# Chunk attention and two feed-forward layers: token blocks of 4x512 + 256 in place of 6x384, first block in one pass, two product buffers

## The chip, the core and the metric

The kernel runs on one core of one Trainium2 chip. The metric is the device time of a run in microseconds (us), shown as the median of three runs. A profiled execution of the same program gives the rows below; its span is counted from the first to the last instruction.

The engines are PE (TensorE, matrix products; PEld are its weight loads), DVE (VectorE), ACT (ScalarE), POOL (GpSimd) and SP, which issues the DMA transfers. Each engine works through its own list of instructions in order, and they meet at semaphores.

## What is computed

There are 2304 tokens (4 sequences of 576), 512 features and 2048 hidden features. Attention is local: each chunk of 64 tokens sees itself alone, with 8 heads of 64 features. Two feed-forward layers follow, the first with softplus, the second with a rational function.

```python
scores = scale * np.matmul(q_c, k_c.transpose(0, 1, 2, 4, 3))   # chunks of 64 tokens
attn = np.exp(scores - scores.max(-1)); attn = attn / (attn.sum(-1) + 1e-09)
x = np.matmul(attn, v_c)                      # -> (2304, 512)
h = x @ w_in                                  # (2304, 2048), layer one
x = (np.maximum(h, 0) + np.log1p(np.exp(-np.abs(h)))) @ w_out
h = x @ w_in2                                 # layer two
P = a[0] + a[1]*h + a[2]*h**2 + a[3]*h**3
Q = 1.0 + abs(b[0])*abs(h) + abs(b[1])*h**2
out = (P / (Q + 1e-6)) @ w_out2
```

## The kernel before

**Products.** Each operand of a product is held as a rounded part and a remainder, and a product is three terms (TERMS): rounded with rounded, rounded with remainder, remainder with rounded. The hidden features are cut into 16 chunks of 128 (fc), the tokens into 6 blocks of T = 384 (three tiles of 128 each). A step s is one chunk of one block. In products_h (L719) it has 12 matmuls of 384 columns into a PSUM tile h. From h, the engines make g, the activation split in two parts: in layer one, softplus twice on ACT (L753 the whole, L758 the rounded part) and a subtraction on POOL (L761); in layer two the rational function on ACT and DVE, then the copy on ACT (L284) and the subtraction on POOL (L292) of split. Then come the output products: products_out1 (L858), 12 matmuls of 384 columns, or products_out2 (L886), 9 matmuls of 512 columns, since in layer two a matmul takes 128 tokens as weights and the 512 output features as columns. They add up in PSUM over the 16 chunks.

**Buffers.** The pool gpool holds three tiles g, ps_h two tiles h, raw four tiles for loads. PSUM holds two sums of 2x512 columns (ps_acc) and one such tile for attention (ps_att). In layer two the attention tile becomes the third sum and one of the two places for the squares.

**Weights.** They lie in memory as 64-bit floats. For each chunk, w_in's and w_out's 512 KB are loaded, scaled down on ACT (L342, "magnitudes"), put together on DVE (L348, L357) and split (L284 on ACT or L286 on POOL, then L292 on DVE). The magnitudes of layer one need another ACT table than softplus has, so each pair of weights costs two table loads (L258).

**Passes.** Blocks 0 and 1 go through layer one in half passes of 8 chunks (HALF): block 0 with chunks 0 to 7, block 1 with the same, then both with chunks 8 to 15. The sums of the first half go to memory (part) and are added in evac1 after the second.

**Attention.** Tiles 0 to 2 are worked on before the first step; tiles 0 to 5 are loaded early into places that weights take later. Their q, k and probabilities are transposed on PE (L491, L591) and copied by ACT (L503, L615). Tiles 6 to 17 are transposed on DVE in 32x32 blocks (L516, L606; 32 instructions a tile), and are worked on during the steps of the blocks ahead of theirs.

**Order.** The program writes down tasks with costs and dependencies (add), and Program.schedule sets each engine's order by them: a list scheduler that goes backward and forward some rounds and keeps its best. The costs only set the order. Dummy matmuls (keep_warm, L1142) fill PE's planned gaps before the first step.

Of the kernel before, what the change touches and what calls it, by code (L numbers as in the profile page):

```python
# [11 lines left out]
F32 = mybir.dt.float32  # L12
# [11 lines left out]
T = 384  # L24
HALF = 8
# [4 lines left out]
CONVERTED = (1,)  # L30
# [5 lines left out]
DIVIDE_BY_POOL = set()  # L36
E_BY_VECTOR = set(range(6, 18))


class Program:  # L40
# [15 lines left out]
    def __init__(self):  # L56
        self.tasks, self.deps, self.table, self.part = [], [], [], ("", 0)
        self.writer, self.readers, self.last_alloc = {}, {}, {}
# [128 lines left out]
def tile_chunk_attention_two_ffn(  # L187
# [30 lines left out]
    NB = NT // T  # L218
    NTB = T // TB
# [16 lines left out]
    att_stack = ctx.enter_context(ExitStack())  # L236
    ps_att = att_stack.enter_context(tc.tile_pool(name="ps_att", bufs=1, space=PSUM))
# [9 lines left out]
    HEAD = 4 * HALF  # L247
# [67 lines left out]
    def prepare(name, after, signed):  # L315
        layer, which, fc = name
        prog.part = f"convert {layer}", f"{which}{fc}"
# [52 lines left out]
    def complete(name, rkey, mkey, shift, merge, signed):  # L370
        layer, which, fc = name
        prog.part = f"convert {layer}", f"{which}{fc}"
# [23 lines left out]
    def reload_w(which, fc):  # L396
# [4 lines left out]
        prog.part = "reload", f"{which}{fc}"  # L401
# [27 lines left out]
    BY_VECTOR = 2 * NTB  # L429
    EARLY = 2 * NTB  # L430
    qk_t, v_t, room = {}, {}, {}

    def attention(tb):
        first = tb < NTB
        j, part = divmod(tb, NTB)
        prog.part = "attention", tb
        qkey = turn("wi", FC) if tb < EARLY else turn("raw", 4)
        vkey = turn("wo", FC) if tb < EARLY else "v"
# [3 lines left out]
        def load_qk(n):  # L442
# [3 lines left out]
            def f():  # L446
                if tb >= EARLY and n == 0:
                    qk_t[tb] = raw.tile([P, H, 2, D], F32, tag="raw", name=f"qk_{tb}")
                for off, m, b, s in runs(tb * TB, TB):
                    if tb < BY_VECTOR:  # L450
# [15 lines left out]
        def load_v():  # L466
            if tb >= EARLY:
                v_t[tb] = att1.tile([P, H, D], F32, tag="v", name=f"v_{tb}")
# [178 lines left out]
        name = min(tb, NTB)  # L647
        ke = ("e", name)
        ka = ("aT", name)
        km, ks = turn("mx", 4), turn("sm", 4)  # L650
        turned = [("turned", name, n) for n in range(16)]
        for n in range(2):
# [3 lines left out]
                alloc=None if tb < EARLY else "raw",  # L656
            )
        qks = [qkey, (qkey, 0), (qkey, 1)]
        if tb < BY_VECTOR:
            for n in range(2):  # L660
# [6 lines left out]
                    turned[8 * n : 8 * n + 8] if n else turned,  # L667
                    alloc=None if first else "qkT",
                )
        else:  # L670
            for n in range(16):
                add(
                    DVE, 0.45, turn_blocks(n // 8, n // 4 % 2, n // 2 % 2, n % 2), qks,
                    [turned[n]] if n else turned, alloc="qkT",
# [12 lines left out]
        if tb in DIVIDE_BY_POOL:  # L687
            add(POOL, 1.0, divide, [ke, ks], [ke])
        else:
            add(DVE, 0.6, divide, [ke, ks], [ke])  # L690
        if tb in E_BY_VECTOR:
            kas = [(ka, n) for n in range(16)]
            for n in range(16):
                add(
                    DVE, 0.315, turn_e_blocks(n // 4, n % 4), [ke],
                    [kas[n]] if n else [ka, *kas], alloc="aT",
                )
        else:
            kas = [ka]
            add(PE, 0.46, turn_e, [ke], [b0])  # L700
            add(ACT, 0.48, take_e, [b0], [ka], alloc="aT")
        add(PE, 0.78, values, [ka, *kas, (vkey, 0)], [b0, b1])
# [6 lines left out]
    def products_h(layer, s, fc, j):  # L709

        key = turn("h", 2)
        prog.part = "h" if s < HEAD else "later h", s

        def f():
            ps = ps_h.tile([P, 512], F32, tag="h", name=f"h_{layer}_{s}")
            hs[s] = ps[:, :T]
# [8 lines left out]
        parts = range(NTB) if layer == 1 else range(KC)  # L725
        reads = [(wk, 0), (wk, 1)] + [((xkey[layer, j], c), n) for c in parts for n in range(2)]
        add(PE, 2.085, f, reads, [key], alloc="h")
        return key

    def scratch(s):  # L730
        t = {}

        def new(tag):
            t[tag] = tmp.tile([P, T], F32, tag=tag, name=f"{tag}_{s}")
# [4 lines left out]
    def split_g(s, t, key, reads):  # L739
        def alloc():  # L740
            gs[s] = gpool.tile([P, 2, T], F32R, tag="g", name=f"g_{s}")

        split(lambda n: gs[s][:, n], lambda: t["t2"], ACT, POOL, T, reads, key, "g", alloc)

    def softplus(s, hkey):

        t, new = scratch(s)
        prog.part = "g" if s < HEAD else "later g", s
        kl, kg = turn("t2", 2), turn("g", 3)
# [5 lines left out]
        def hi():  # L755
            table(SOFTPLUS)
            gs[s] = gpool.tile([P, 2, T], F32R, tag="g", name=f"g_{s}")
            act.activation(gs[s][:, 0], hs[s], AF.Softplus)  # L758

        def lo():  # L760
            pool.tensor_tensor(  # L761
                out=gs[s][:, 1], in0=t["t2"], in1=gs[s][:, 0].bitcast(F32), op=ALU.subtract
            )

        add(ACT, 0.37, whole, [hkey], [kl], alloc="t2", table=SOFTPLUS)
        add(ACT, 0.37, hi, [hkey], [(kg, 0)], alloc="g", table=SOFTPLUS)
        add(POOL, 1.09, lo, [kl, (kg, 0)], [(kg, 1)])
        return kg

    def rational(s, hkey, start=None):  # L770

        t, new = scratch(s)
        prog.part = "g" if s < HEAD else "later g", s
        ku = ("att", 1) if s % 2 == 0 else (x["ukey"], 0)
        kd, kp, kg = turn("t1", 2), turn("t2", 2), turn("g", 3)
        bring = {0: "att", 1: "acc"}.get(start)  # L780

        def u():
            return (x["even"] if s % 2 == 0 else x["u"][:, 0])[:, :T]

        def square():
            if bring == "att":
                att_stack.close()
                ps_two = ctx.enter_context(tc.tile_pool(name="ps_two", bufs=1, space=PSUM))
                for what in ("third", "even"):
                    x[what] = ps_two.tile([P, 512], F32, tag=what, name=what)  # L790
            if bring == "acc":
                x["u"] = ps_acc.tile([P, 2, 512], F32, tag="acc", name="u")
# [25 lines left out]
        add(
            ACT, 0.56,
# [366 lines left out]
```

## Time and profile before

| what | value |
|---|---|
| median of the runs | 894.42 us (894.19 to 894.69) |
| span of the profiled execution | 892.4 us |
| PE busy | 868.6 us (97%), 5642 matmuls |
| PEld busy | 811.7 us (91%) |
| DVE busy | 680.2 us (76%) |
| ACT busy | 522.5 us (59%), of it 44.9 us in 35 table loads |
| POOL busy | 269.2 us (30%) |
| DMA | 74.38 MB, mean 83 GB/s |

The run is 2.0 us longer than the span of the profiled execution. Matmuls are pipelined: each is shown some 340 ns long, while the next begins 173 ns after it, so the pace is read from the starts. A busy PE is therefore not yet PE at its pace. Wait tables name who released an engine last.

### The profile page before, as it was taken

What the parts mean: (1) busy time and instruction counts of PE and PEld (TensorE: products, weight loads), DVE (VectorE), ACT (ScalarE), POOL (GpSimd) and SP (SyncE); (2) the same over time, 40 slices, a digit from 0 to 9 for tenths busy, and PEclk for the clock granted to TensorE, in tenths of its full rate; (3) what the DMA queues carried; (4) which work ended last, traced back from release to release, by engine and by line L of the source; (5) the groups of instructions that cost most, each with busy time, mean ns of one, the idle gap of its engine ahead of it and who ended that gap; (6) DMA issues with size and microseconds to landing.
All of it is one profiled execution on the core that took longest, in us unless ns stands there. A gap on an engine that the chain in (4) does not pass through costs nothing. (4 is left out here: it accounts for less than half of the span.)

```text
span 892.4 us, 14897 instructions
## 1 busy us (share of the span) xinstructions
PE 868.6 (97%) x5642; PEld 811.7 (91%) x5642; DVE 680.2 (76%) x1326; ACT 522.5 (59%) x991; POOL 269.2 (30%) x278
## 2 busy tenths in 40 slices
PE   8898999999999999999998999999999999999997
PEld 7788999999999999999997889898889888888996
DVE  4686679899779969922598887877787687787885
ACT  4799972243233333234447877766677767776774
POOL 0124431222122122215334935225224225222221
PEclk9999999999999999999999999999999999999999
DMA  9755573141443434134353412002000000000000
GB/s 189 212 179 206 179 206 84 48 119 40 116 118 95 108 94 131 49 118 139 122 175 123 134 54 71 1 1 69 3 1 24 12 1 1 36 1 1 36 0 36
DMA packets 77353, 74.38 MB, mean 83 GB/s; under 512 B 34272, under 2 KB 62944, under 8 KB 77280
## 3 DMA queue, kind: packets, MB, share of 16 engines
q1 hardware_dynamic: 77280, 73.42, 28.4%
q8 instruction: 44, 0.72, 0.4%
q14 instruction: 29, 0.24, 0.1%
HBM read 58.20 MB, written 15.20 MB: 82 GB/s over the span
## 5 line engine op out<-in xcount | busy, mean ns | idle before, releaser
L858 PE MATMUL acc<-g,w_1o 128*128 128x384 f32 x1152 | 218.2, 337 | 3.7 <-POOL g L761 3.3
L719 PE MATMUL h<-xT,w_2i 128*128 128x384 f32 x1152 | 216.5, 337 | 1.9 <-DVE t L796 1.8
L719 PE MATMUL h<-xT,w_1i 128*128 128x384 f32 x1152 | 213.2, 336 | 2.7 <-ACT w_1i L284 2.7
L719 PEld LDWEIGHTS h<-xT,w_2i 128*128 128x128 f32 x1152 | 204.0, 188 | 11.2 <-DVE t L796 5.0
L858 PEld LDWEIGHTS acc<-g,w_1o 128*128 128x128 f32 x1152 | 200.5, 188 | 6.0 <-POOL g L761 3.8
L719 PEld LDWEIGHTS h<-xT,w_1i 128*128 128x128 f32 x1152 | 199.9, 188 | 4.5 <-ACT w_1i L284 3.6
L761 POOL TENSOR_TENSOR g<-t,g 128x384 fp32r<-128x384 f32 x96 | 103.0, 1073 | 272.7 <-ACT g L758 206.3
L292 POOL TENSOR_TENSOR g<-t,g 128x384 fp32r<-128x384 f32 x96 | 97.9, 1020 | 253.5 <-ACT g L284 191.5
L886 PE MATMUL acc<-w_2o,g 128*128 128x512 f32 x576 | 148.4, 392 | 0.9 <-POOL g L292 0.6
L886 PEld LDWEIGHTS acc<-w_2o,g 128*128 128x128 f32 x576 | 107.4, 188 | 23.0 <-POOL g L292 0.9
L753 ACT ACTIVATE t<-h 128x384 f32<-128x384 f32 x96 | 46.8, 490 | 101.5 <-PE h L719 96.5
L758 ACT ACTIVATE g<-h 128x384 fp32r<-128x384 f32 x96 | 47.1, 490 | 70.2 <-PE acc L858 52.8
L516 DVE STREAM_TRANSPOSE qkT<-qk 32x256 f32<-32x256 f32 x192 | 83.8, 436 | 4.8 <-PE aps L534 1.2
L886 PE MATMUL third<-w_2o,g 128*128 128x512 f32 x288 | 82.8, 394 | 1.4 <-POOL g L292 1.4
L284 ACT ACTIVATE g<-t 128x384 fp32r<-128x384 f32 x96 | 50.0, 521 | 45.9 <-DVE t L796 42.1
L829 DVE TENSOR_TENSOR t<-h,t 128x384 f32<-128x384 f32 x96 | 53.2, 554 | 26.2 <-ACT t L815 13.8
L820 ACT ACTIVATE t<-h,na_t 128x384 f32<-128x384 f32 x96 | 64.2, 669 | 12.2 <-PE h L719 7.0
L796 DVE SCALAR_TENSOR_TENSOR t<-t,na_t,h 128x384 f32<-128x384 f32 x96 | 58.7, 612 | 12.6 <-ACT t L815 4.0
L886 PEld LDWEIGHTS third<-w_2o,g 128*128 128x128 f32 x288 | 53.1, 188 | 10.9 <-POOL g L292 2.8
L815 ACT ACTIVATE t<-h,b_t 128x384 f32<-128x384 f32 x96 | 54.9, 573 | 9.8 <-PE h L719 6.2
L606 DVE STREAM_TRANSPOSE aT<-e 32x128 f32<-32x128 f32 x192 | 58.1, 303 | 3.1
L258 ACT ACT_TABLE_LOAD x35 | 44.9, 1283 | 1.3 <-PEq L1167 0.7
(92 smaller groups left out, 914.9 us busy)
## 6 DMA issues: line engine op xcount, KB each, us to landing
wr_1i<-in_moe_w_in_dram SPq DMA_DIRECT2D x16, 512.0 KB, 3.8
wr_1o<-in_moe_w_out_dram SPq DMA_DIRECT2D x16, 512.0 KB, 4.4
wr_2i<-in_moe_w_in_dram SPq DMA_DIRECT2D x16, 512.0 KB, 3.9
wr_2o<-in_moe_w_out_dram SPq DMA_DIRECT2D x16, 512.0 KB, 4.3
x<-x2s SPq DMA_DIRECT2D x12, 384.0 KB, 2.7
x2r<-x SPq DMA_DIRECT2D x12, 384.0 KB, 3.3
out_dram<-o SPq DMA_DIRECT2D x18, 256.0 KB, 2.1
qk<-in_q_dram SPq DMA_DIRECT2D x16, 256.0 KB, 5.1
```

The source lines that it names most:

```text
L284: act.activation(d, s, AF.Copy)
L292: eng.tensor_tensor(out=dst(1), in0=src(), in1=dst(0).bitcast(F32), op=ALU.subtract)
L516: vec.transpose(tiles["qkT"][p0 : p0 + 32, n, :, c * CH : (c + 1) * CH].rearrange("p g (u t) -> p g t u", t=2), qk_t[tb][p1 : p1 + 32, h:: ...
L606: vec.transpose(o[32 * k : 32 * k + 32, :, 32 * p : 32 * p + 32], e[32 * p : 32 * p + 32, :, 32 * k : 32 * k + 32],)
L719: pe.matmul(hs[s], w[:, a, c * P : (c + 1) * P], xt[:, b, c, :], start=n == 0, stop=n == 3 * KC - 1,)
L761: pool.tensor_tensor(out=gs[s][:, 1], in0=t["t2"], in1=gs[s][:, 0].bitcast(F32), op=ALU.subtract)
L796: return lambda: vec.scalar_tensor_tensor(out=out(), in0=in0(), scalar=scalar, in1=in1(), op0=op0, op1=op1)
L815: ACT, 0.465, lambda: (table(EXP_LN), act.activation(new("t1"), h(), AF.Abs, scale=b_t[:, 0:1])),
L820: lambda: act.activation(new("t2"), h(), AF.Identity, scale=na_t[:, 3:4], bias=na_t[:, 2:3]),
L829: DVE, 0.47, lambda: vec.tensor_tensor(out=p(), in0=h(), in1=p(), op=ALU.mult),
L858: pe.matmul(accs[run, half][:, c % 2, :T], wts[1, "o", fc][:, a, c * P : (c + 1) * P], gs[s][:, b, :], start=first and n == 0, stop=last a ...
L886: pe.matmul(sum2(j, c), gs[s][:, b, c * P : (c + 1) * P], wts[2, "o", fc][:, a, :], start=first and n == 0, stop=last and n == 2,)
```

## The change

The tokens are cut into four blocks of 512 and one of 256 (tokens 2048 to 2303, attention tiles 16 and 17). Layer one takes them in the order 0, 4, 1, 2, 3, layer two in 0, 1, 4, 2, 3. Each block goes through all 16 chunks at once; the half passes, their sums in memory and the additions are gone. Tiles 0 to 3 come before the first step, 16 and 17 are the other two that are loaded early. The tiles transposed by DVE are 6 to 15 (ten in place of twelve); 4, 5, 16 and 17 are transposed by PE. gpool has two tiles in place of three. The results of a sum go out through tiles of the raw pool, 2x512 at a time, in place of a tile of their own (iop). In layer two the squares lie in the attention tile, and both sums of ps_acc hold two token tiles each. Later attention tiles use the pool of the activations (tmp, t1). A step's output products are put on the scheduler's list one step after it in place of two; the costs of tasks follow the block's size.

```diff
-T = 384
-HALF = 8
+T = 512
+BLOCKS = ((0, 512), (512, 512), (1024, 512), (1536, 512), (2048, 256))
+ORDER1 = (0, 4, 1, 2, 3)
+ORDER2 = (0, 1, 4, 2, 3)
-E_BY_VECTOR = set(range(6, 18))
+STARTING = (0, 1, 2, 3)
+STAGED = (0, 1, 2, 3, 16, 17)
+QK_BY_VECTOR = set(range(6, 16))
+E_BY_VECTOR = set(range(6, 16))
...
-    gpool = ctx.enter_context(tc.tile_pool(name="gpool", bufs=3))
+    gpool = ctx.enter_context(tc.tile_pool(name="gpool", bufs=2))
-    iop = ctx.enter_context(tc.tile_pool(name="iop", bufs=1))
...
     def products_h(layer, s, fc, j):
         key = turn("h", 2)
+        n_tok = BLOCKS[j][1]
...
-                    hs[s], w[:, a, c * P : (c + 1) * P], xt[:, b, c, :],
+                    hs[s], w[:, a, c * P : (c + 1) * P], xt[:, b, c, :n_tok],
...
+    def evacuate(layer, j, half, n, store, store_cost, outs):
+        name = layer, j, half
+        key = turn("raw", 4)
...
-    passes = [
-        (0, range(0, HALF), 0),
-        (1, range(0, HALF), 0),
-        (0, range(HALF, FC), 1),
-        (1, range(HALF, FC), 1),
-    ] + [(j, range(FC), 2) for j in range(2, NB)]
...
+    for bi, j in enumerate(ORDER1):
+        last_block = bi == len(ORDER1) - 1
+        coming = [] if last_block else [t for t in tiles_of(ORDER1[bi + 1]) if t not in STAGED]
...
+            if coming and fc % 4 == 0:
+                attention(coming.pop(0))
...
             hkey = products_h(1, s, fc, j)
             steps.append(len(prog.tasks) - 1)
-            gkey = softplus(s, hkey)
+            if len(outs) > 1:
+                outs.pop(0)()
+            gkey = softplus(s, hkey, j)
...
-            if len(outs) > 2:
-                flush()
```

DVE before the first step: in the kernel before, one weight and the products xT of tiles 1, 2 (aps_1, aps_2) and 3, which belongs to block 1 (xT_1).

```order
L584 TENSOR_TENSOR e_3_362<-e_3_362,sm_3_388 128x512
L292 TENSOR_TENSOR xT_0_283<-aps_2_215,xT_0_283 128x4x128
L348 TENSOR_SCALAR cm_1i_0_448<-cm_1i_0_448 128x512
L292 TENSOR_TENSOR xT_1_450<-aps_3_309,xT_1_450 128x4x128
L357 SCALAR_TENSOR_TENSOR cm_1i_0_448<-wr_1i_0_385,cm_1i_0_448 128x512
L292 TENSOR_TENSOR w_1i_0_126<-cm_1i_0_448,w_1i_0_126 128x512
```

The same place now:

```order
L584 TENSOR_TENSOR room_3_1_137<-room_3_1_137,sm_3_389 128x512
L351 TENSOR_SCALAR cm_1i_0_393<-cm_1i_0_393 128x512
L360 SCALAR_TENSOR_TENSOR cm_1i_0_393<-wr_1i_0_344,cm_1i_0_393 128x512
L296 TENSOR_TENSOR w_1i_0_120<-cm_1i_0_393,w_1i_0_120 128x512
L296 TENSOR_TENSOR xT_0_290<-aps_2_246,xT_0_290 128x4x128
L296 TENSOR_TENSOR xT_0_290<-aps_3_311,xT_0_290 128x4x128
```

The weight's three instructions stand ahead of the last two products, and all four products belong to block 0, whose first step reads them.

PE where the first half pass ended; h_1_8 is layer one, step 8, w_1i_0 the first chunk of w_in, acc_0_0 the first sum of the first pass:

```order
L719 MATMUL h_1_7_931<-xT_0_283,w_1i_7_133 128x384 x12
L858 MATMUL acc_0_0_569<-g_6_922,w_1o_6_929 128x384 x6
L719 MATMUL h_1_8_963<-xT_1_450,w_1i_0_126 128x384 x12
L719 MATMUL h_1_9_985<-xT_1_450,w_1i_1_127 128x384 x12
L719 MATMUL h_1_10_1011<-xT_1_450,w_1i_2_128 128x384 x12
L858 MATMUL acc_0_1_586<-g_6_922,w_1o_6_929 128x384 x6
```

The same steps now:

```order
L716 MATMUL h_1_7_923<-xT_0_290,w_1i_7_127 128x512 x12
L863 MATMUL acc_1_0_0_547<-g_6_918,w_1o_6_916 128x512 x6
L863 MATMUL acc_1_0_1_561<-g_6_918,w_1o_6_916 128x512 x6
L716 MATMUL h_1_8_972<-xT_0_290,w_1i_8_128 128x512 x12
L863 MATMUL acc_1_0_1_561<-g_7_967,w_1o_7_965 128x512 x6
L863 MATMUL acc_1_0_0_547<-g_7_967,w_1o_7_965 128x512 x6
```

Step 8 went back to the first chunk with another block's tokens; now it takes the ninth chunk (w_1i_8) for the same block, and each step's output products stand one step behind it.

PE in layer two, third block, before:

```order
L719 MATMUL h_2_139_6929<-xT2_2_5858,w_2i_11_5287 128x384 x12
L886 MATMUL third_5197<-w_2o_8_5156,g_136_6908 128x512 x3
L886 MATMUL acc2_5328<-w_2o_8_5156,g_136_6908 128x512 x6
L719 MATMUL h_2_140_6971<-xT2_2_5858,w_2i_12_5376 128x384 x12
L886 MATMUL acc2_5328<-w_2o_9_5235,g_137_6944 128x512 x6
```

And in the block of 256 now:

```order
L716 MATMUL h_2_118_6269<-xT2_4_5540,w_2i_6_4386 128x256 x12
L889 MATMUL acc_2_4_0_6175<-w_2o_3_4254,g_115_6249 128x512 x6
L716 MATMUL h_2_119_6306<-xT2_4_5540,w_2i_7_4437 128x256 x12
L889 MATMUL acc_2_4_0_6175<-w_2o_4_4307,g_116_6282 128x512 x6
L716 MATMUL h_2_120_6343<-xT2_4_5540,w_2i_8_4495 128x256 x12
```

A step's output products still stand three steps behind it, with two buffers g; the matmuls of a step are 12 of 256 and 6 of 512 columns.

## Rows read from the trace of the kernel before

**Rows 1.** Stretches of the span: PE, PEld, DVE, ACT, POOL busy; clock; DMA.

```profile
33.70:90.00 56.30, 49.98 (x363) 46.19 (x360) 42.53 (x70) 53.15 (x78) 18.88 (x20) 1.00 0.57 190
...
120.00:188.80 68.80, 68.43 (x575) 66.01 (x573) 62.77 (x147) 25.17 (x45) 16.98 (x17) 1.00 0.33 86
...
440.00:500.00 60.00, 56.48 (x303) 54.05 (x302) 54.92 (x87) 39.12 (x78) 29.48 (x29) 0.97 0.48 150
500.00:886.60 386.60, 383.65 (x1915) 344.51 (x1915) 301.30 (x552) 276.33 (x560) 127.36 (x135) 1.00 0.07 23
```

**Rows 2.** PE in order of time, first 70 us, attention and the first step.

```profile
29.84 1.04 PE L491 MATMUL aps<-ident,qk 128*128 128x128 f32 x8
30.71 1.06 PE L1142 MATMUL warm<-ident 128*128 128x128 f32 x8
32.63 1.15 PE L534 MATMUL aps<-qkT 64*64 64x64 f32 x32 [0.86 <-ACT qkT L503]
33.71 4.49 PE L719 MATMUL h<-xT,w_1i 128*128 128x384 f32 x24
...
62.22 0.69 PE L622 MATMUL aps<-aT,v 64*64 64x64 f32 x32
62.85 2.35 PE L719 MATMUL h<-xT,w_1i 128*128 128x384 f32 x12
```

**Rows 3.** The chain that ended last, at its end: start, its share of time, instructions.

```profile
863.15 1.36 PE acc L886 x6
...
886.60 0.61 ACT o L978
```

**Rows 4.** PE in order of time, layer one: start, length, instructions; starts give the pace.

```profile
265.42 2.24 PE L719 MATMUL h<-xT,w_1i 128*128 128x384 f32 x12
267.50 2.24 PE L858 MATMUL acc<-g,w_1o 128*128 128x384 f32 x12
```

**Rows 5.** Matmuls by line and shape, 33.7 to 90 us: busy, mean ns, idle before.

```profile
L719 PE MATMUL h<-xT,w_1i 128*128 128x384 f32 x144 | 27.3, 340 | 2.7 <-ACT w_1i L284 2.7
L858 PE MATMUL acc<-g,w_1o 128*128 128x384 f32 x103 | 20.7, 341 | 1.4 <-POOL g L761 1.2
```

**Rows 6.** The same view, 500 to 886.6 us.

```profile
L719 PE MATMUL h<-xT,w_2i 128*128 128x384 f32 x1080 | 202.1, 337 | 1.6 <-DVE t L796 1.6
L886 PE MATMUL acc<-w_2o,g 128*128 128x512 f32 x558 | 143.7, 392 | 0.9 <-POOL g L292 0.6 <-DVE o L980 0.3
L886 PE MATMUL third<-w_2o,g 128*128 128x512 f32 x277 | 79.5, 394 | 0.4 <-POOL g L292 0.4
```

**Rows 7.** All engines in order of time, just before the first step.

```profile
28.05 0.69 DVE L292 TENSOR_TENSOR xT<-aps,xT 128x512 fp32r<-128x512 f32 x1 [0.42 <-ACT xT L284]
28.66 0.68 DVE L357 SCALAR_TENSOR_TENSOR cm_1i<-wr_1i,cm_1i 128x512 uint32<-128x512 uint32 x1
...
31.47 0.62 ACT L284 ACTIVATE w_1i<-cm_1i 128x512 fp32r<-128x512 f32 x1
...
32.13 0.69 DVE L292 TENSOR_TENSOR w_1i<-cm_1i,w_1i 128x512 fp32r<-128x512 f32 x1 [2.79 <-ACT w_1i L284]
```

**Rows 8.** ACT in order of time, one round of converting weights (two table loads).

```profile
68.84 1.28 ACT L258 ACT_TABLE_LOAD   x1
...
73.09 0.49 ACT L758 ACTIVATE g<-h 128x384 fp32r<-128x384 f32 x1
...
74.11 1.28 ACT L258 ACT_TABLE_LOAD   x1
```

**Rows 9.** ACT by line, 500 to 880 us: one copy of 512 columns.

```profile
L978 ACT ACTIVATE o<-acc 128x512 f32<-128x512 f32 x5 | 3.0, 598 | 0.0
```

**Rows 10.** POOL by line, 500 to 880 us: a subtraction of 512 columns.

```profile
L292 POOL TENSOR_TENSOR w_2o<-w2r_o,w_2o 128x512 fp32r<-128x512 f32 x4 | 5.2, 1300 | 0.0
```

**Rows 11.** Groups of instructions over the whole span: DVE's transposes of q and k.

```profile
L516 DVE STREAM_TRANSPOSE qkT<-qk 32x256 f32<-32x256 f32 x192 | 83.8, 436 | 4.8 <-PE aps L534 1.2
```

**Rows 12.** Who PE waited for, 440 to 500 us: us, times, longest.

```profile
PE acc L858 <- POOL g L761: 2.0, 1, 2.0
```

More of the change, by code (lines that the diff above doesn't have):

```diff
@@ L428, in tile_chunk_attention_two_ffn @@
     xkey = {}
-    BY_VECTOR = 2 * NTB
-    EARLY = 2 * NTB
+    room_key = {}
     qk_t, v_t, room = {}, {}, {}
     def attention(tb):
[L434 to L438, printed above, removed]
+        first = tb in STARTING
+        staged = tb in STAGED
+        qk_by_vector = tb in QK_BY_VECTOR
+        j, part = divmod(tb, T // TB)
+        qkey = turn("wi", FC) if staged else turn("raw", 4)
+        vkey = turn("wo", FC) if staged else "v"
         ps = {}
@@ L724, in products_h, with scratch, new_g, softplus @@
         wk = wkey[layer, "i", fc]
-        parts = range(NTB) if layer == 1 else range(KC)
+        parts = range(n_tok // TB) if layer == 1 else range(KC)
         reads = [(wk, 0), (wk, 1)] + [((xkey[layer, j], c), n) for c in parts for n in range(2)]
-        add(PE, 2.085, f, reads, [key], alloc="h")
+        add(PE, 3 * KC * (n_tok + 32) / 2400, f, reads, [key], alloc="h")
         return key
-    def scratch(s):
+    def scratch(s, n_tok):
         t = {}
         def new(tag):
-            t[tag] = tmp.tile([P, T], F32, tag=tag, name=f"{tag}_{s}")
+            t[tag] = tmp.tile([P, T], F32, tag=tag, name=f"{tag}_{s}")[:, :n_tok]
             return t[tag]
         return t, new
[L739 to L749, printed above, removed]
+    def new_g(s):
+        gs[s] = gpool.tile([P, 2, T], F32R, tag="g", name=f"g_{s}")
+    def softplus(s, hkey, j):
+        n_tok = BLOCKS[j][1]
+        t, new = scratch(s, n_tok)
+        kl, kg = turn("t2", 2), turn("g", 2)
         def whole():
@@ L875, in products_out2, with f @@
         wk = wkey[2, "o", fc]
-        prog.part = "out" if s < HEAD else "later out", s
-        if first and j == 0:
-            accs["key"] = turn("acc", 2)
-        def f(tiles):
-            def g():
-                if first and j == 0 and tiles[0] == 0:
-                    accs[2] = ps_acc.tile([P, 2, 512], F32, tag="acc", name="acc2")
-                for c in tiles:
+        for half in range(BLOCKS[j][1] // (2 * TB)):
+            def f(half=half):
+                if first:
+                    new_acc(2, j, half)
+                for c in (2 * half, 2 * half + 1):
                     for n, (a, b) in enumerate(TERMS):
                         pe.matmul(
-                            sum2(j, c),
+                            accs[2, j, half][:, c % 2],
                             gs[s][:, b, c * P : (c + 1) * P],
@@ new lines, in products_out2, with move @@
+            keys = [(acckey[2, j, half], 0), (acckey[2, j, half], 1)]
+            add(
+                PE, 6 * (DM + 32) / 2400, f,
+                [(gkey, 0), (gkey, 1), (wk, 0), (wk, 1)] + ([] if first else keys), keys,
+                alloc="acc" if first else None,
+            )
+    x2d = [
+        dpool.tile([P, KC, n], F32, tag=f"x2_{j}", name=f"x2_{j}")
+        for j, (_, n) in enumerate(BLOCKS)
+    ]
+    ev = {}
+    def evacuate(layer, j, half, n, store, store_cost, outs):
+        name = layer, j, half
+        key = turn("raw", 4)
+        for c in range(2):
+            def move(c=c):
@@ L941, in f @@
                 if c == 0:
-                    new()
-                if c % 2 == 0:
+                    ev[name] = raw.tile([P, 2, n], F32, tag="raw", name="ev_%d_%d_%d" % name)
+                src = accs[name][:, c, :n]
+                if c == 0:
                     act.activation(ev[name][:, c], src, AF.Copy)
@@ L998, in reload_x2, with evac1, store @@
-    def reload_x2(j, half):
+            add(
+                DVE if c else ACT, on_dve(n) if c else on_act(n), move, [(acckey[name], c)],
+                [(key, c)] if c else [key, (key, 0), (key, 1)], alloc=None if c else "raw",
+            )
+        for cs, out_key in outs:
+            add(
+                DMA, store_cost, lambda cs=cs: store(ev[name], cs),
+                [key, *((key, c) for c in cs)], [out_key],
+            )
+    def evac1(j):
+        for half in range(2):
+            def store(tile, cs, half=half):
+                sync.dma_start(out=x2d[j][:, 2 * half : 2 * half + 2], in_=tile)
+            evacuate(1, j, half, BLOCKS[j][1], store, 2.0, [((0, 1), ("x2", j, half))])
@@ L1000, in reload_x2, with evac2, store @@
+    def evac2(j):
+        t0, n = BLOCKS[j]
+        for half in range(n // (2 * TB)):
+            def store(tile, cs, half=half):
+                t = t0 + (2 * half + cs[0]) * P
+                sync.dma_start(out=out[t : t + P, :], in_=tile[:, cs[0]])
+            evacuate(
+                2, j, half, DM, store, 0.95, [((c,), ("out", j, half, c)) for c in range(2)]
+            )
+    def reload_x2(j, half, on_act_dve):
         key = turn("raw", 4)
-        prog.part = "x2", j
+        n_tok = BLOCKS[j][1]
```

344 lines of the change are left out of this document (134 added, 210 removed).

## The prediction

> **What bounds the kernel now.** I read the stretches first. PE is busy in 99% of 120 to 188.8 us and of 500 to 886.6 us; from 33.7 to 90 us it is busy for 49.98 of 56.30, and there ACT is busy for 53.15 [rows 1]. So PE sets the end, but for the head, where attention (up to 33.71 us, when the first step starts [rows 2]) and then ACT set it. The last matmul ends at 886.60 and the span 5.8 us later [rows 3]. So the kernel is priced by PE's pace, and what PE loses is found by subtraction.
>
> The pace: 12 matmuls of 384 columns start 2.08 us apart (265.42 to 267.50 [rows 4]), 173.3 ns each. Six of 512 columns take 1.36 us [rows 3], 226.7 ns each. The 128 further columns cost 53.4 ns, so the first 384 would be 160 ns at that slope and 13.3 ns are left that a matmul costs whatever its width. This is the center of the case: fewer, wider matmuls save 13.3 ns apiece.
>
> The sum of before: 6 blocks x 16 chunks x 36 matmuls = 3456 of 384 columns x 173.3 ns = 598.9 us, and 864 of 512 x 226.7 = 195.9: 794.8 us. Attention on PE, from starts: q and k transposed 0.87 us a tile (29.84 to 30.71), scores 1.08 (32.63 to 33.71), values 0.63 (62.22 to 62.85) [rows 2], and the transposes of the probabilities, four for the eight of q and k, 0.43. A tile that DVE transposes costs 1.71 us, one that PE transposes 3.01. After the first step come the rest of tile 4 (1.06), tile 5 and twelve of the cheap kind (20.5): 24.6. From 33.7 to 886.6 are 852.9 us, so **PE loses 33.5 us** to waits, changes of work and slower stretches. Of them 56.3 - 247 x 0.1733 - 4.1 = 9.4 lie before 90 us [rows 1, 5]; 386.6 - 1080 x 0.1733 - 835 x 0.2267 = 10.1 after 500 us [rows 1, 6]; 14.0 between.
>
> **The change, part by part.**
>
> *Matmuls.* Layers one and two now have 16 x 36 matmuls in each of five blocks: 2304 of 512 columns x 226.7 = 522.3 us and 576 of 256. The last are not in this trace. By the two prices above they cost 13.3 + 106.7 = 120 ns: 69.1 us. From below they are bounded by 128 columns with a weight load each, 0.87/8 = 109 ns [rows 2], from above by the straight line from that to 173.3 at 384, which is 141. I take 120, on the line of the two rows with whole streams. The 864 of layer two stay. **Gain 794.8 - 787.3 = 7.5 us** (bounds 13.8 and, at 141, a loss of 4.6).
>
> The Trainium skill (TensorE: Matmul & The Clock Gate, Back-to-back issue gap) gives N/2.4 + 2.5 ns for a warm matmul, 162.5 for 384 columns and 215.8 for 512. This trace has 173.3 and 226.7 [rows 3, 4]: the slope agrees, the floor does not. By the page's floor the gain would be 576 x 2.5 ns = 1.4 us.
>
> *Attention on PE.* Only ten tiles are left to DVE, and 4, 5, 16, 17 go to PE. After the first step come tile 16 less half its first transposes (2.57), three of 3.01 and ten of 1.71: 28.7. **Loss 4.1 us.** DVE gets rid of two tiles' 64 transposes, which buys nothing directly, since PE sets the end there.
>
> *Head.* Four tiles must be done before the first step, not three. But before, four were done too: DVE starts the fourth's last product at 28.05 and ends it at 28.74. The first step waited on for its weight: ACT split it at 31.47 and DVE at 32.13 [rows 7], behind tile 4's copies. Now DVE's shift, merge and split of that weight stand ahead of the last two products (the order of DVE), some 0.6 + 0.6 + 0.4 = 1.6 us more in its queue after 28.7, and the weight's load stands 14th in SP's list, not 16th. First step at 30.3 in place of 33.7: **gain 3.4 us** (bounds 5.0, if the weight hides, and 0, if the fourth tile's own chain slips).
>
> *First pass.* This is the largest part. A round of ACT (two table loads, two magnitudes, two softplus, a split) lasts 74.11 - 68.84 = 5.27 us and brings one chunk of weights [rows 8]. In before that chunk brings PE 24 x 173.3 = 4.16 us of work; until block 1's tokens joined, PE was starved by 1.1 us a chunk, and so idled for the weights (2.7 us) and for POOL [rows 5]. With 512 tokens the chunk brings 24 x 226.7 = 5.44 us of work, and the round grows by two softplus of 128 more columns, 0.11 each (598 ns [rows 9] against 490 [rows 8]), to 5.49. The two are level: 0.05 x 16 = 0.8 us lost. Tiles 16 and 17 put some 2.6 us each on ACT there and about as much on PE. Filling the pipe of the first step (softplus, then POOL 1.3 us [rows 10]) costs some 2 more. I take 3 in place of 9.4: **gain 6.4 us** (bounds 8.6 and 0). The half passes' stores, reloads and additions go; they lay beside PE's work and I cost them nothing.
>
> *The narrow block in layer one* has 16 x 24 x 0.120 = 46 us of steps and 7.5 of attention on PE. DVE has to do in it 46 transposes of q and k (tiles 6, 7 and most of 8) x 0.436 = 20 us [rows 11], 32 smaller ones of probabilities, at most 14, and for four tiles five instructions of 512 columns at 0.69 [rows 7] and two short ones, 3.8 a tile: 49 us at most, 92% of it. From 120 to 188.8 us DVE was busy for 62.77 of 68.8 and PE still for 68.43 [rows 1], so it is tight but hidden. If it were not, PE would wait before the next block, a few us once.
>
> *Middle and change of layers.* 14.0 us were lost, among them 2.0 for one subtraction behind a weight on POOL [rows 12] and a stretch at a mean clock of 0.97 [rows 1], 1.8 us of 60 there. Every block's end is a place to lose, and there are fewer. I take 10: **gain 4 us** (bounds 8 and -4). The results' new place, the raw pool, shares four tiles with weights and tokens, and SP waits in order for a free one; the loads' lead hides that; without it a load's whole time would show.
>
> *Layer two.* I leave the 10.1 us lost as they are. A step of the narrow block has 12 x 120 + 6 x 226.7 = 2.80 us of PE. The two buffers g: the copy into one must wait until the products two steps earlier are done; then come the copy (0.6 us) and POOL (1.3) [rows 9, 10], with their hops some 2.2 us. Between those products and their own, PE has a step of h and one of output products, 5.44 us, in the narrow block two of h and one, 4.2. So it is hidden while ACT and POOL come at once; POOL was busy for 127 of 386.6 us [rows 1].
>
> The sum: 892.4 - 7.5 + 4.1 - 3.4 - 6.4 - 4 = 875.2; with the tail unchanged and the 2.0 us by which the median stands above the span, **877 us**.
>
> **The rivals.**
>
> *Slower: two product buffers are too few.* Whenever the copy into g or POOL comes over 3.2 us late (5.44 less 2.2), PE stands. All 160 steps pay. At 0.15 us a step that is 24 us: 877 + 24 = 901. It decides from 17.4/160 = 0.11 us a step. Against it: PE waited for POOL's g for some 1 us in all of 500 to 886.6 [rows 6], and POOL is at a third. For it: those waits were with three buffers.
>
> *ACT keeps the first pass.* If a round takes 5.9 us (attention's copies between the table loads, DVE's splits late), 16 x 0.4 = 6.4 us are lost again: 883.4.
>
> *Narrow matmuls cost 141 ns*, since each waits for its weights: 877 + 12.1 = 889. PEld was busy for 66.01 of 68.8 us at 384 columns [rows 1]; against it stands the 109 ns.
>
> *The cost of a matmul goes by its columns*, with no fixed 13.3 ns: 226.7/512 = 0.443 ns a column, 173.3/384 = 0.451. Then there is hardly a gain in matmuls: 877 + 7.5 = 884.5. The two rows speak against it. The rule of the Trainium skill weighed above (TensorE: Matmul & The Clock Gate, Back-to-back issue gap) stands nearest to it; with its floor the time would be 883.
>
> *Better:* the fewer ends of blocks also help layer two, and the middle loses little: 868.
>
> **How the numbers follow.** The forecast (870 to 882) gets 0.58, better 0.08, ACT 0.12, narrow 0.07, columns 0.05, two buffers 0.10. A measurement can tell 0.2% (1.8 us) from no change. Slower needs the buffers: 0.08, with 0.02 of them near 894. Of the narrow rival 0.02, with another loss beside it, falls there too: same 0.04, faster 0.88. The range 867 to 892 takes in all but the buffers and half of the better case; it spans the bounds of the first pass (6.4), of the narrow matmuls (12.1) and of the middle.
>
> **What would show it.** Starts of 512-column matmuls 227 ns apart in layer one, of 256 ones 120: the matmul term. The first step near 30 us: the head. ACT's table loads 5.5 us apart and PE idle for under 3 us up to some 125 us: the first pass. PE's waits for POOL's or ACT's g of over 5 us after 480 us, or PE busy under 97% in the block of 256, would speak for the buffers. I am wrong if PE's pace at 512 is not 227, or if the scheduler's order, made with its own costs, leaves waits that I did not read in it.

## The result: slower, and layer two lost it

The changed kernel takes 906.2 us (median; 905.4 to 906.9) where the kernel before takes 894.6: a ratio of 1.0131, 95% interval 1.0117 to 1.0145. The forecast was 877, the range 867 to 892. The span of the profiled execution went from 892.4 to 903.6 us.

The stretches of the changed kernel come first: the first block, the narrow block, the rest of layer one, and then layer two's five blocks in their order 0, 1, narrow, 2, 3, each from its first matmul of h to that of the next (columns as in [rows 1]). Only the first border, 127.0, lies 1.3 us behind the narrow block's first matmul (125.67).

```profile
29.90:127.00 97.10, 95.48 (x575) 77.60 (x574) 68.25 (x112) 90.27 (x120) 35.52 (x32) 1.00 0.59 176
127.00:184.60 57.60, 56.77 (x627) 54.38 (x626) 42.52 (x102) 19.79 (x45) 11.78 (x16) 1.00 0.20 52
184.60:460.00 275.40, 273.77 (x1643) 222.90 (x1642) 206.77 (x422) 102.86 (x176) 83.10 (x66) 1.00 0.42 123
460.00:554.90 94.90, 90.03 (x385) 71.44 (x384) 64.38 (x94) 62.76 (x103) 34.36 (x30) 1.00 0.10 34
554.90:645.20 90.30, 86.89 (x380) 70.76 (x379) 66.87 (x97) 58.44 (x96) 24.77 (x24) 1.00 0.05 18
645.20:702.90 57.70, 51.50 (x302) 42.08 (x300) 41.26 (x94) 38.45 (x94) 19.43 (x23) 1.00 0.18 56
702.90:795.80 92.90, 88.14 (x373) 70.54 (x374) 68.71 (x105) 61.57 (x105) 27.56 (x25) 0.98 0.02 6
795.80:897.80 102.00, 97.37 (x412) 79.20 (x411) 70.79 (x102) 61.93 (x102) 23.23 (x18) 0.97 0.03 11
```

Layer one is full: PE is busy for 426.0 of 430.1 us. Layer two's first matmul starts at 460.0, where before it started at 470.7, so 10.7 us had been gained by then. Layer two then lasts 437.8 us to 897.8, against 415.9 before (470.7 to 886.6). In the narrow block PE is busy for 51.50 of 57.70 us, 89%, while DVE (41.26) and ACT (38.45) are not busy either. No engine is the bound there: they wait for each other.

PE by line and shape in layer two, 480 to 897.8 us, answers to [rows 6]:

```profile
L889 PE MATMUL acc<-w_2o,g 128*128 128x512 f32 x853 | 212.7, 397 | 12.4 <-POOL g L809 5.4 <-ACT g L806 4.3 <-DVE ev L924 2.7
L716 PE MATMUL h<-xT,w_2i 128*128 128x512 f32 x720 | 174.6, 393 | 6.0 <-DVE t L779 6.0
L716 PE MATMUL h<-xT,w_2i 128*128 128x256 f32 x192 | 26.8, 289 | 4.7 <-DVE t L779 4.5
```

PE idles for 23.1 us before these, against 2.9 in [rows 6]. For 9.7 of them it waits for g, which is what the rival "two product buffers are too few" had named as its sign, and for 10.5 for DVE, which is late in reading h.

Who waits for whom among ACT and DVE, 480 to 898 us (us in total, times, longest):

```profile
DVE t L779 <- ACT u L776: 28.4, 30, 2.6
DVE t L779 <- ACT u L802: 26.2, 33, 2.5
ACT u L776 <- DVE t L779: 25.3, 29, 2.3
ACT u L798 <- DVE t L779: 22.0, 32, 2.1
...
ACT u L776 <- DVE u L779: 11.0, 13, 1.9
```

These rows lead to the cause. u is the PSUM place in which ACT puts a step's squares (L776), then the logarithm (L798) and its exponential (L802), and which DVE reads and writes in between (L779). The square needs h from PE and its own half, which the step two before it has left. Yet ACT waited 36 us with it for DVE's L779. In the kernel before, 500 to 887 us, the same wait was 0.3 us in all:

```profile
ACT u L793 <- DVE t L796: 0.3, 1, 0.3
```

Both kernels have two places, for even and for odd steps. Before, they were two tiles (`x["even"]` and `x["u"][:, 0]`); the change made them the two halves of one tile, `x["u"][:, s % 2]`, each half a PSUM bank of its own. The prediction did not speak of this line of the diff.

All engines in order of time in the changed kernel, two steps k and k+1 of block 2 (PEld, POOL and SP left out):

```profile
773.04 0.69 ACT L798 ACTIVATE u<-t,epsq_t 128x512 f32<-128x512 f32 x1 [0.38 <-DVE t L779]
773.77 0.58 ACT L776 ACTIVATE u<-h 128x512 f32<-128x512 f32 x1
774.38 0.58 ACT L802 ACTIVATE u<-u 128x512 f32<-128x512 f32 x1
...
775.00 0.75 DVE L779 SCALAR_TENSOR_TENSOR t<-u,absb_t,t 128x512 f32<-128x512 f32 x1 [1.99 <-ACT u L802]
...
775.67 0.74 DVE L779 SCALAR_TENSOR_TENSOR t<-t,epsq_t,u 128x512 f32<-128x512 f32 x1
...
776.44 0.69 ACT L798 ACTIVATE u<-t,epsq_t 128x512 f32<-128x512 f32 x1 [0.79 <-DVE t L779]
777.16 0.58 ACT L802 ACTIVATE u<-u 128x512 f32<-128x512 f32 x1
777.78 0.76 DVE L779 SCALAR_TENSOR_TENSOR u<-t,na_t,u 128x512 f32<-128x512 f32 x1 [0.77 <-ACT u L802]
...
780.53 0.58 ACT L776 ACTIVATE u<-h 128x512 f32<-128x512 f32 x1
...
780.56 0.50 PE L889 MATMUL acc<-w_2o,g 128*128 128x512 f32 x1 [2.38 <-ACT g L806]
...
781.14 0.75 DVE L779 SCALAR_TENSOR_TENSOR u<-t,na_t,u 128x512 f32<-128x512 f32 x1 [0.71 <-ACT u L776]
```

The reader is to see the turns. DVE's operation at 775.00 belongs to step k+1 and needs the square that ended at 774.35. It starts at 775.00, when the exponential of step k, on the other half, has ended (774.96). The logarithm of step k+1 at 776.44 has its input at 775.75 and waits for DVE's operation on step k, which ends at 776.41. The operation at 777.78 works on step k, whose exponential ended at 774.96; it waits for that of step k+1 (777.74). The one at 781.14 waits for the square of step k+2 (780.53 to 781.11), though it works on the half of k+1. In these rows each access to the tile stands behind the other engine's last access to it, whichever half that touched, and at the end PE stands for 2.38 us.

### The profile page after: what moved, and what is told of

Read it like the earlier page. It is cut to its first block, busy times and chain, and to the rows that moved or that the text cites. A ratio compares the mean times of both kernels' runs of the same rounds, so it can differ in the third digit from the quotient of the medians.

```text
span 903.6 us, 13458 instructions
## 1 busy us (share of the span) xinstructions
PE 868.2 (96%) x5090; PEld 714.0 (79%) x5090; DVE 647.6 (72%) x1159; ACT 511.8 (57%) x864; POOL 260.4 (29%) x238
## 4 chain that ended last, share of the span: by engine, by line
PE 58%; DVE 23%; ACT 14%; issue 3%; DMA 0%; POOL 0%; ACTq 0%; DVEq 0%; POOLq 0%
PE h L716 26%; PE acc L863 18%; DVE t L779 13%; PE acc L889 8%; DVE u L779 4%; ACT u L776 3%; ACT u L798 3%; PE aps L536 2%; ACT u L802 2%; DVE t L832 2%; ACT g L806 2%; ACT t L794 2%; PE warm L1085 1%; PE aps L622 1%; DVE qkT L518 1%
## 5 line engine op out<-in xcount | busy, mean ns | idle before, releaser
L889 PE MATMUL acc<-w_2o,g 128*128 128x512 f32 x864 | 215.6, 397 | 12.6 <-POOL g L809 5.4
L716 PE MATMUL h<-xT,w_2i 128*128 128x512 f32 (+1 forms) x960 | 213.0, 372 | 11.3 <-DVE t L779 11.0
L716 PE MATMUL h<-xT,w_1i 128*128 128x512 f32 (+1 forms) x960 | 211.3, 371 | 2.2 <-ACT g L751 1.6
L863 PE MATMUL acc<-g,w_1o 128*128 128x512 f32 (+1 forms) x960 | 211.0, 370 | 0.0
L889 PEld LDWEIGHTS acc<-w_2o,g 128*128 128x128 f32 x864 | 162.8, 191 | 51.6 <-POOL g L809 7.9
L716 PEld LDWEIGHTS h<-xT,w_1i 128*128 128x128 f32 x960 | 166.7, 189 | 33.7 <-ACT g L751 2.5
L809 POOL TENSOR_TENSOR g<-t,g 128x512 fp32r<-128x512 f32 (+1 forms) x80 | 94.3, 1179 | 302.1 <-ACT g L806 282.5
L754 POOL TENSOR_TENSOR g<-t,g 128x512 fp32r<-128x512 f32 (+1 forms) x80 | 102.5, 1282 | 226.4 <-ACT g L751 209.9
L779 DVE SCALAR_TENSOR_TENSOR t<-u,absb_t,t 128x512 f32<-128x512 f32 (+1 forms) x80 | 55.5, 694 | 42.0 <-ACT t L794 18.2
L779 DVE SCALAR_TENSOR_TENSOR t<-t,epsq_t,u 128x512 f32<-128x512 f32 (+1 forms) x80 | 55.4, 693 | 22.1 <-ACT u L802 17.0
L798 ACT ACTIVATE u<-t,epsq_t 128x512 f32<-128x512 f32 (+1 forms) x80 | 52.0, 650 | 32.6 <-DVE t L779 23.9
L776 ACT ACTIVATE u<-h 128x512 f32<-128x512 f32 (+1 forms) x80 | 43.2, 540 | 44.8 <-DVE t L779 26.2
L779 DVE SCALAR_TENSOR_TENSOR u<-t,na_t,u 128x512 f32<-128x512 f32 (+1 forms) x80 | 55.9, 699 | 15.1 <-ACT u L776 11.5
L821 ACT ACTIVATE t<-h,na_t 128x512 f32<-128x512 f32 (+1 forms) x80 | 58.6, 732 | 7.0 <-PE h L716 6.2
L779 DVE SCALAR_TENSOR_TENSOR t<-t,na_t,h 128x512 f32<-128x512 f32 (+1 forms) x80 | 55.4, 693 | 9.3 <-ACT t L794 4.5
```

The costliest lines, as they stand in the source:

```text
L716: pe.matmul(hs[s], w[:, a, c * P : (c + 1) * P], xt[:, b, c, :n_tok], start=n == 0, stop=n == 3 * KC - 1,)
L754: pool.tensor_tensor(out=gs[s][:, 1, :n_tok], in0=t["t2"], in1=gs[s][:, 0, :n_tok].bitcast(F32), op=ALU.subtract,)
L776: act.activation(u(), h(), AF.Square)
L779: return lambda: vec.scalar_tensor_tensor(out=out(), in0=in0(), scalar=scalar, in1=in1(), op0=op0, op1=op1)
L798: act.activation(u(), d(), AF.Ln, bias=epsq_t)
L809: pool.tensor_tensor(out=gs[s][:, 1, :n_tok], in0=p(), in1=gs[s][:, 0, :n_tok].bitcast(F32), op=ALU.subtract,)
```

## The experiments

**Theory A**: the shared tile, as just read. **Theory B**: two product buffers g. **Theory D**: a step of 512 tokens has a chain of operations too long for two steps in flight.

**e1: two u tiles.** The tiles take the two banks that the shared tile had.

```
...
-            return x["u"][:, s % 2, :n_tok]
+            return x["u", s % 2][:, :n_tok]
...
-                x["u"] = ps_att.tile([P, 2, 512], F32, tag="att", name="u")
+                att_stack.close()
+                ps_two = ctx.enter_context(tc.tile_pool(name="ps_two", bufs=1, space=PSUM))
+                for n in range(2):
+                    x["u", n] = ps_two.tile([P, 512], F32, tag=f"u{n}", name=f"u{n}")
```

> The changed kernel with one edit: the place for the squares, the logarithms and the reciprocals of layer two (u) is two tiles of one PSUM bank each, one for even steps and one for odd, in place of one tile of two banks. Every instruction stands in the same order on every engine; only the waits differ. Theory A (the shared tile: an instruction on the odd step's half waits for the last one on the even step's half, so the two chains of operations take turns between ACT and DVE): layer two loses about as much as before the change, 20 of its 45 us, so 906 - 25 = 881 us (876 to 888), DVE's waits for u fall by more than half. Theory B (two product buffers): at most 1 us less, 904 to 907. Theory D (a step of 512 tokens simply has a longer chain of operations than two steps' depth can hide): 898 to 907.

Measured: 871.5 us (871.4 to 871.6), 0.9744 of before (0.9729 to 0.9758): 34.7 us below the changed kernel and 4.5 us under the range that theory A had named. Its layer two in stretches (blocks 0, 1, narrow, 2), and who PE waits for from 480 to 864.4 us:

```profile
460.10:547.10 87.00, 87.00 (x385) 72.05 (x384) 64.50 (x96) 62.55 (x104) 35.58 (x30) 1.00 0.11 37
547.10:633.60 86.50, 86.04 (x379) 70.87 (x378) 65.17 (x95) 57.26 (x94) 23.67 (x23) 1.00 0.05 19
633.60:682.50 48.90, 48.15 (x301) 43.24 (x300) 40.66 (x95) 37.96 (x96) 19.44 (x23) 1.00 0.21 66
682.50:768.50 86.00, 84.87 (x373) 69.74 (x372) 67.84 (x103) 60.74 (x106) 27.78 (x26) 1.00 0.02 7
```

```profile
L893 PE MATMUL acc<-w_2o,g 128*128 128x512 f32 x849 | 205.5, 390 | 3.4 <-POOL g L813 1.7 <-DVE ev L928 1.5 <-ACT g L810 0.2
L717 PE MATMUL h<-xT,w_2i 128*128 128x512 f32 x720 | 172.0, 389 | 0.5 <-DVE t L783 0.5
L717 PE MATMUL h<-xT,w_2i 128*128 128x256 f32 x192 | 25.5, 283 | 0.0
```

PE's idle time falls from 23.1 to 3.9 us, with ACT and DVE about as busy as with the shared tile. DVE's waits for ACT's u fall from 79 to 47 us, not by the half that A expected; ACT's waits with u for DVE fall from 75 to 18 us, and the square's 36 to 0.4 (sums of the waits of 480 us to the end, in both kernels). The same two steps as above, the same operations in the same order:

```profile
749.05 0.69 ACT L802 ACTIVATE u<-t,epsq_t 128x512 f32<-128x512 f32 x1 [0.38 <-DVE t L783]
...
749.68 0.55 ACT L780 ACTIVATE u<-h 128x512 f32<-128x512 f32 x1
750.15 0.56 ACT L806 ACTIVATE u<-u 128x512 f32<-128x512 f32 x1
750.26 0.75 DVE L783 SCALAR_TENSOR_TENSOR t<-u,absb_t,t 128x512 f32<-128x512 f32 x1 [1.25 <-ACT u L780]
...
752.18 0.75 DVE L783 SCALAR_TENSOR_TENSOR u<-t,na_t,u 128x512 f32<-128x512 f32 x1
...
754.96 0.49 PE L893 MATMUL acc<-w_2o,g 128*128 128x512 f32 x1 [0.21 <-ACT g L810]
```

DVE's operation at 750.26 now starts when its own square has ended (750.23), beside the exponential. From the logarithm to PE's matmul are 5.91 us, where 7.52 were (773.04 to 780.56). The instructions stand in the same order on every engine and the data in the same banks, so only the waits differ: theory A is shown, and D falls, for the long steps now run at PE's pace, 87.0 us for 16.

The Trainium skill (PSUM — Partial Sum Buffer, PSUM bank collisions raise a hardware error) asks for semaphores between engines by bank and quadrant of partitions, not by address. Two banks then need none between them; e1 without those waits agrees, and the waits of the shared tile came from the way the program was written.

**e2: the kernel before, with the sharing.**

```
-            return (x["even"] if s % 2 == 0 else x["u"][:, 0])[:, :T]
+            return (x["even"] if start == 0 else x["u"][:, 1 - s % 2])[:, :T]
```

> The kernel before with one edit: from the second even step of layer two on, the even steps' squares lie in the free second bank of the tile that holds the odd steps', so that both share one tile. The order of instructions is the same on every engine. Theory A: slower, by 10 to 30 us (905 to 925); the same turns between ACT and DVE show. Theories B and D: 894 to 896.

Measured: 948.0 us, 1.0597 of before (1.0581 to 1.0612): more than A expected. One block of layer two, in the kernel before and then in e2:

```profile
677.90:746.20 68.30, 68.11 (x340) 60.84 (x339) 53.19 (x99) 47.20 (x97) 21.12 (x23) 1.00 0.03 12
```

```profile
700.00:778.20 78.20, 70.97 (x340) 60.56 (x341) 54.98 (x99) 49.60 (x99) 22.29 (x25) 1.00 0.03 11
```

The sharing costs the old blocks 53 us and the new ones 35. So the rest of the change is worth far more than it seemed: 894.6 to 871.5 with u apart on both sides.

**e3: a third product buffer** for the changed kernel, in layer two.

```
...
-        gs[s] = gpool.tile([P, 2, T], F32R, tag="g", name=f"g_{s}")
+        own = (att1, "qkT") if third else (gpool, "g")
+        gs[s] = own[0].tile([P, 2, T], F32R, tag=own[1], name=f"g_{s}")
...
-            new_g(s)
+            new_g(s, s % 3 == 1)
```

> The changed kernel with one edit: in layer two every third product tile g lies in a tile of the attention that is free by then, so layer two has three product buffers; u stays one shared tile and the order of instructions is the same on every engine. Theory B: 878 to 890 us. Theory A: 902 to 907, since the chains still take turns. Theory D: 902 to 907.

Measured: 905.5 us (902.5 to 907.1). PE's waits are as they were:

```profile
L890 PE MATMUL acc<-w_2o,g 128*128 128x512 f32 x855 | 212.9, 396 | 12.4 <-POOL g L810 5.2 <-ACT g L807 4.3 <-DVE ev L925 2.7
```

PE waits for g, but not because g has no room: g's content is late. Theory B falls for layer two.

**e4 and e6: two product buffers in the kernel before, and its listing alone.** Two buffers need the output products listed one step earlier; e6 has that listing with three buffers.

```
-    gpool = ctx.enter_context(tc.tile_pool(name="gpool", bufs=3))
+    gpool = ctx.enter_context(tc.tile_pool(name="gpool", bufs=2))
...
+            if len(outs) > 1:
+                flush()
             gkey = softplus(s, hkey)
...
-            if len(outs) > 2:
-                flush()
```

(In both layers. e4 also has `turn("g", 2)` in place of `turn("g", 3)`, so that the planner knows of two buffers; e6 keeps the 3 and is without the first two lines.)

> The kernel before with two product buffers in place of three, in both layers, and the output products of a step listed one step earlier, as two buffers need; blocks of 384 tokens, and u and even apart, as before. Theory B: slower by 8 to 25 us (902 to 920). Theory A: 893 to 898 us. Theory D says nothing of it beyond 893 to 900.

> The kernel before with three product buffers, as it had, and only the listing of e4_before_two_g: a step's output products stand one step earlier in the list that the planner starts from. If the 11 us of e4 come from that listing and the order the planner makes of it: 902 to 908 us. If they come from the buffers: 893 to 897.

Measured: e4 905.8 us (ratio 1.0113 to 1.0143), e6 898.2 (1.0036 to 1.0070). By the number, e4 came out as theory B had said (902 to 920), and not as A and D had. Neither expectation of e6 was met; it lies between. The listing costs 4 us, the buffers and the order that the planner makes of them another 7.5. It is not PE waiting for g, as B would have it: from the first step on PE waited 2.4 us for g in e4 and 5.5 in the kernel before. In e4 layer two starts 9.7 us late (480.4), and its loss in layer one lies at 110 to 264 us, around attention. There, up to 194 us, PE waited for DVE's transposed probabilities (2.7 us), and from 151.7 to 193.7 the clock was 0.92. Since the planner's order changes with the buffers, what two of them cost at 384 tokens by themselves stays open.

**e5: two u tiles and a third product buffer**, known to the planner too (the edits of e1 and e3, with a key of its own for the third).

> Two u tiles as in e1_u_apart, and a third product buffer in layer two as in e3_after_third_g, here also known to the planner, so that some instructions of layer two are placed anew. Layer two of e1 loses about 5 us to stalls. If two product buffers are what is left of them: 866 to 868 us. If not (theory A is the whole of it): 870 to 873.

Measured: 872.8 us (872.4 to 873.2), no less than e1. With u apart, a third buffer brings the new blocks nothing in the order that the planner makes with it.

**e7: two u tiles, the narrow block last in layer two.** `ORDER2 = (0, 1, 2, 3, 4)` in place of `(0, 1, 4, 2, 3)`.

> Two u tiles as in e1_u_apart, and layer two's block of 256 tokens last in place of third. In e1 that block takes 48.9 us where its products alone are 44.8, and behind the last block PE waits for the last steps' chains. A shorter last chain: 868 to 871 us. If the narrow block's own loss only moves to the end: 871 to 874.

Measured: 869.2 us (869.2 to 869.5), 0.9721 of before (0.9705 to 0.9737). It was run once more:

> The kernel of e7_u_apart_narrow_last once more, beside e8 and e10 on one chip: 868.5 to 870.5 us.

Measured: 869.6 (869.4 to 869.8). This is the best version, 2.8% below before and 2 us below e1 (the intervals of their ratios overlap a little).

**e8: the shared tile with six accesses in place of seven.** If the turns are the cost, a shorter row of them must cost less.

```
-        add(DVE, on_dve(n_tok, 1), stt(u, p, na_t[:, 0:1], u, ALU.add, ALU.mult), [kp, ku], [ku])
-        add(DVE, on_dve(n_tok), stt(p, d, 2.0, u, ALU.subtract, ALU.mult), [ku, kd], [kp])
+        add(DVE, on_dve(n_tok, 1), stt(p, p, na_t[:, 0:1], u, ALU.add, ALU.mult), [kp, ku], [ku])
+        add(DVE, on_dve(n_tok), stt(p, d, 2.0, p, ALU.subtract, ALU.mult), [ku, kd], [kp])
```

> The changed kernel, u still one shared tile, the order of instructions the same; but the last two operations of a step on DVE pass their value through the product's own scratch tile t in place of u, so that six accesses to u are in a row per step, not seven (0.69 us less of 512 columns). If the accesses to the shared tile, taken in turn, are what a step lasts (theory A, read as a chain: 4.8 us of instructions on u and some time between them, 5.8 us measured a step where PE needs 5.44): most of the 0.4 us a step comes back, 878 to 895 us. If the sharing costs for another reason than the length of that chain: 902 to 907.

Measured: 892.2 us (891.8 to 893.3), 14 us of the 35 given back with as many instructions. Its layer two:

```profile
460.80:553.40 92.60, 89.28 (x386) 71.48 (x385) 64.97 (x94) 62.25 (x103) 34.73 (x30) 1.00 0.11 35
553.40:642.60 89.20, 86.58 (x380) 70.75 (x379) 68.89 (x97) 58.65 (x97) 25.82 (x24) 1.00 0.06 18
642.60:695.70 53.10, 49.31 (x301) 42.70 (x299) 41.46 (x94) 38.22 (x94) 19.80 (x23) 1.00 0.19 60
695.70:787.20 91.50, 87.72 (x372) 70.68 (x373) 69.29 (x105) 61.37 (x105) 28.59 (x25) 0.98 0.02 6
```

The narrow block gains 4.6 us and the three wide ones 1.1 to 2.3; the last block, not shown, gains another 4.8 up to its last matmul. Some 3 of the 14 us are not the turns themselves but a clock that fell once in place of three times (last section). The direction is A's and the total in its range. "Most of the 0.4 us a step" was wrong for the wide steps: over blocks 0, 1 and 2 they went from 5.79 to 5.69 us, with 5.44 as PE's own.

**e10: the same edit on e7.**

> Two u tiles, the narrow block last (e7_u_apart_narrow_last), and the value passed through t as in e8_shared_one_less. With u apart no turns are left to shorten: theory A expects no change against e7, 868 to 870 us.

Measured: 873.4 us (873.2 to 873.8), 4 more where none were expected. All of it lies in block 0 of layer two (90.9 us against 87.0). DVE and POOL there, in order of time, and the wait of PE behind them:

```profile
497.04 1.29 POOL L813 TENSOR_TENSOR g<-t,g 128x512 fp32r<-128x512 f32 x1 [1.35 <-ACT g L810]
...
497.59 1.29 DVE L783 SCALAR_TENSOR_TENSOR t<-t,t 128x512 f32<-128x512 f32 x1
...
503.06 0.67 PE L717 MATMUL h<-xT,w_2i 128*128 128x512 f32 x1 [1.89 <-DVE t L783]
```

The edit gives DVE's last operation two tensors in SBUF (t and t), where u had been in PSUM. Beside a POOL instruction it then lasts 1.08 us in the mean (17 of 64, up to 1.66), alone 0.69; with u in PSUM it lasts 0.68 either way (e7 run again, 17 and 47). The Trainium skill (SBUF — State Buffer, Who interferes with whom) says so: a DVE instruction with two SBUF inputs contends with a GpSimd one that reads SBUF. The same tax lies in e8 (12 of 64 beside POOL, 0.98 us in the mean). DVE is late by it and reads h late; PE waits for 1.89 us and runs the 3 us from 503.4 at clock 0.50. That the two slow operations ahead make this one wait was not tried apart.

**How long the turns are.** The seven accesses to u of one step last 0.58 + 0.75 + 0.69 + 0.58 + 0.75 + 0.75 + 0.69 = 4.79 us at 512 tokens, and by the same seven rows 3.08 at 256 in the changed kernel and 3.9 at 384 in the kernel before. With the tile shared, a step took 5.79 (three blocks), 3.61 (57.7/16) and 4.83 us (e2, 64 steps from 546.8 to 855.6): 1.2 times each of them, where PE alone needs 5.44, 2.80 and 4.12. Read so, a shared tile puts a floor under the step that is made of ACT's and DVE's lengths in series, which no busy share shows, and the new blocks' larger PE time hides more of it than the old blocks', which fits their smaller loss. But the 1.2 is a reading of three widths, not a rule that was tested, and e8 does not keep to it: its six accesses last 4.10 us, 1.2 times that would be 4.9, under PE's 5.44, and the step took 5.69.

## The prediction, step by step

What PE lost is here the sum, over all matmuls, of the time from a matmul's start to the next one's beyond its pace.

- **Matmuls (-7.5): right.** In layer one 18 narrow ones take 2.16 us, 120 ns each, and 12 wide ones 2.72, 226.7 (PE in order of time):

```profile
153.93 2.32 PE L863 MATMUL acc<-g,w_1o 128*128 128x256 f32 x18
156.09 2.08 PE L716 MATMUL h<-xT,w_1i 128*128 128x256 f32 x16
```

```profile
285.85 2.88 PE L716 MATMUL h<-xT,w_1i 128*128 128x512 f32 x12
288.57 2.88 PE L863 MATMUL acc<-g,w_1o 128*128 128x512 f32 x12
```

The rivals "narrow" and "columns" fall with these, and so does, for this stream, the floor of 2.5 ns that the Trainium skill (TensorE: Matmul & The Clock Gate, Back-to-back issue gap) gives for an isolated warm matmul: 256 columns would be 109 ns by it.

- **Attention (+4.1): too high.** After the first step PE spends 28.1 us on it (forecast 28.7), but before it had spent 26.7, not 24.6. The loss is 1.4, and what I had too little there stood in the middle term.
- **Head (-3.4): right.** The first step starts at 29.91, 3.8 us earlier.
- **First pass (-6.4): right but for 1 us.** ACT's table loads, one round apart, stand at 71.03 and 76.50, 5.47 us (forecast 5.49). PE loses 4.2 us up to 125.7, against 9.6 up to 109.6 before: a gain of 5.4. The rival "ACT keeps the first pass" falls. The narrow block behind it hid its attention, as forecast: PE was busy for 56.77 of 57.60 us.

```profile
71.03 1.28 ACT L256 ACT_TABLE_LOAD   x1
...
76.50 1.28 ACT L256 ACT_TABLE_LOAD   x1
```

- **Middle and change of layers (-4): 1.4** (10.5 lost from 125.7 to 480, against 11.9 from 109.6 to 500). With attention's 1.4 it comes to nothing, as I had it.
- **Layer two (0): this step failed.** It lost 38.4 us after 480, where the kernel before lost 10.3 by this count (10.1 in the prediction): 28.1 more, where the forecast put nothing. "I leave the 10.1 us lost as they are" rested on a look at g alone. That the two places of u had become one tile was in the diff, and was not priced; e1 shows that the waits it brought are the loss: without them layer two loses 5.9.

The sum with measured terms: 892.4 - 7.5 + 1.4 - 3.8 - 5.4 - 1.4 + 28.1 = 903.8, and the span is 903.6. With u apart (e1) layer two loses 5.9 in place of 10.1, and the span is 869.5 where I had 875.2: with the tile mended, the forecast is 6 us too high, 4 of them in layer two, where the rival "better" had the right idea.

The rival "two product buffers" had the sign, and with 901 nearly the time. Both of its tell-tales came true too: PE's waits for g over 5 us (5.4 for POOL and 4.3 for ACT) and PE under 97% in the narrow block (89%). Yet e3 shows it wrong, so its nearness is luck. Its tell-tales would have come with anything that makes g late, so they could not tell the buffers from what stands ahead of them.

## What to carry to other kernels

When a change puts two buffers into one tile, read that line as an added wait: here every access to one half stood behind the other engine's last access to either, and two chains that had run side by side took turns. Set the lengths in series of a step's accesses to the tile (here 4.8 us) beside the bound engine's time for a step (5.4): where the first comes near the second, as here, a loss can come though it is still the smaller (the step took 5.79), and busy shares of some 70% do not show it. And a wait for a buffer's content is not a want of buffers: here a third buffer, with the order of instructions kept, told the two apart in a single run (e3).

## What the chip showed that I had not expected

A wait of PE can be paid twice. After the idle time at 780 us (2.38 and 0.91 us), and again after 816, the granted clock fell to half, 1.2 GHz, for 3.4 us with PE fully busy. The second place, first with the wait (PE idle for 2.71 us in it), then behind it:

```profile
816.20:820.20 4.00, 1.29 (x6) 0.85 (x5) 2.86 (x5) 3.77 (x8) 1.28 (x1) 1.00 0.34 131
820.30:823.70 3.40, 3.40 (x10) 2.64 (x9) 3.33 (x6) 1.73 (x3) 0.00 (x0) 0.50 0.40 154
```

A matmul of 512 columns took 427 ns there in place of 227, and some eight of them pay, 1.6 us. It happened three times in the changed kernel's layer two (the third time at 892 us, after waits of 1.01 and 0.91), once each in e8 and e10, not in e1's, and in the kernel before once, at the change of layers (475.8 us, after a wait of 2.04). By an estimate from these starts, 3 x 1.6 = 4.8 us of the 28.1 that layer two lost were paid in this way. Not every wait brings it: PE idled for 1.7 us at 575 us and the clock stayed at 1.00.
